# Block-sparse attention with a SoLU feed-forward: moving transposes from TensorE to the DMA crossbar, and the feed-forward to tokens on partitions

## The chip, the cores and the metric

The kernel runs on one core of one Trainium2 chip. The metric is the device time of one execution in microseconds (us), lower is better; the profile's span, from the first to the last instruction, is about 1.7 us shorter. Engines are named as in the profile: PE is TensorE (PEld its weight load), DVE is VectorE, ACT is ScalarE, POOL is GpSimd, SP is SyncE, here the issuer of most DMAs. A run counts as slow when it is more than 1.5 % above the fastest of its kernel. Ratios are those formed from fast runs of the same rounds.

## The reference

```python
# q, k, v: (4 batches, 8 heads, 768 tokens, 64), block = 32
scores = scale * q @ k^T                        # 768 x 768 for each head
scores = where(mask, scores, -1e9)              # window of 1 block, first and last block, 3 random blocks a row
attn   = softmax(scores) @ v
x      = attn, heads side by side               # (3072 tokens, 512)
h      = x @ w_in                               # (3072, 1024)
solu   = h * softmax(h)                         # over the 1024
ln     = (solu - mean) / sqrt(var + 1e-6) * g_ln
out    = ln @ w_out                             # (3072, 512)
```

## The kernel before

Heads go through in pairs ("pr"), queries in tiles of 256 ("t"), so there are 48 attention units, each of three groups of four score matmuls. The mask is added by the score matmul itself: 24 more contraction rows hold block indicators in kT and mask values in qT. One feed-forward ("feed") follows every four units. A small planner inside the kernel simulates the engines with rough costs, decides the order of all operations, and emits them in that order. On the chip each engine then runs its own list in order. `take` draws a buffer from a pool, `last_of` gives it back, `due` is a priority.

The k and q path before: GpSimd casts, TensorE transposes, VectorE copies out of PSUM.

```python
ca = op(e, us, cast, [ld], due=due, take=mp, last_of=[ld])           # e is POOL but for the first pair
def tp(o, cb=cb, ca=ca):
    for c in range(NCH):                                             # 6 transposes by PE
        nc.tensor.matmul(t[:, c * P : (c + 1) * P], cb[ca.slot][:, c], ident, is_transpose=True, ...)
t = op("PE", NCH * 0.056, tp, [ca, mids], due=due, take="m", last_of=[ca])
...
got.append(op(e2, ..., cp, [t, prev], due=due + 0.1, ...))           # PSUM -> kT or qT, one copy a head
```

The feed-forward before: the 1024 features of h lie on partitions, so solu needs no transpose for the output matmul, but the sums over features become 48 narrow matmuls a feed.

```python
xp = op("PE", 2 * KD * 0.056, xpose, x_done[(b, t)], ...)            # x transposed by PE
for f2 in range(KF // 2):                                            # four times
    h  = op("PE",  8 * 0.1088, hmm, [xc, w_in_load], take="m", ...)  # w_in stationary, tokens moving
    e  = op("ACT", act_us(512), ... func=ACT.Exp ...)
    so = op("DVE", dve_us(512), ... tensor_mul ...)                  # solu
    sqs.append(op("DVE", dve_us(512, 2), ... tensor_mul ...))        # squares
st = op("PE", 48 * 0.0256, stats, es + sos + sqs, ...)               # sums of e, solu, solu^2 by matmuls with ones
om = op("PE", KF * 0.2156, outp, sos + wo, ...)                      # twice
```

w_out is prepared on the chip. Eight VectorE operations `wg` scale it by g, TensorE sums its columns (`cs`), and eight more VectorE operations `wo` subtract the mean `wbar`. Every output matmul waits for `wo`.

The softmax here doesn't subtract the row's maximum and nothing guards it: scores larger than these inputs give would overflow.

Of the kernel before, what the change touches and what calls it, by code (L numbers as in the profile page):

```python
# [7 lines left out]
FP32 = mybir.dt.float32  # L8
# [24 lines left out]
class Op:  # L33
    def __init__(self, eng, us, emit, deps, due, take=None, last_of=(), load=None, after=()):
        self.eng, self.us, self.emit, self.due = eng, us, emit, due
        self.deps = [d for d in deps if d is not None]
        self.after = list(after)
        self.take = take
        self.last_of = list(last_of)
        self.load = load  # L40
        self.slot = None
        self.start = None
        self.seen = None


class Plan:


    def __init__(self):
        self.ops = []  # L50
        self.pools = {}
        self.free = {e: 0.8 for e in SEEN}
        self.dma_free = 0.0

    def pool(self, name, n):
        self.pools[name] = [0.0] * n

    def op(self, eng, us, emit, deps=(), due=0.0, take=None, last_of=(), load=None, after=()):
        o = Op(eng, us, emit, deps, due, take, last_of, load, after)
        self.ops.append(o)  # L60
        return o

    def place(self, o, wait=0.03):

        t = 0.0
        for d in o.deps:
            if d.seen is None:
                return INF, None
            t = max(t, d.seen)
        for d in o.after:  # L70
            if d.start is None:
                return INF, None
            t = max(t, d.start)
        slot = None
        if o.take is not None:
            slots = self.pools[o.take]
            slot = min(range(len(slots)), key=lambda k: (slots[k], k))
            t = max(t, slots[slot])
        return t, slot

    def run(self):
        todo = {e: [] for e in SEEN}
        for o in self.ops:
            todo[o.eng].append(o)
        order = []
        while any(todo.values()):
            best = None
            for e, ops in todo.items():
                if not ops:
                    continue  # L90
                now = self.free[e]
                pick = None
                for o in ops:
                    t, slot = self.place(o)
                    if t == INF:
                        continue
                    key = (max(t, now), o.due) if t > now + 0.02 else (now, o.due)
                    if pick is None or key < pick[0]:
                        pick = (key, o, slot, max(t, now))
                if pick is not None and (best is None or pick[3] < best[3]):  # L100
                    best = pick
            assert best is not None, "nothing can be placed"
            _, o, slot, t = best
            todo[o.eng].remove(o)
# [3 lines left out]
            if o.load is not None:  # L108
                self.dma_free = max(self.dma_free, t + 1.0) + o.load
                o.seen = self.dma_free + 1.3  # L110
            if o.take is not None:
                o.slot = slot
                self.pools[o.take][slot] = INF
            for a in o.last_of:
                self.pools[a.take][a.slot] = o.seen
            order.append((t, len(order), o))
        order.sort(key=lambda r: r[:2])
# [4 lines left out]
def kernel(  # L122
# [19 lines left out]
    NT = 3  # L142
# [8 lines left out]
    eps_ln = 1e-6  # L151

# [3 lines left out]
    NST, NKB, NEX, NX, NE, NSO, NSQ, NXT, NOT = 3, 3, 9, 6, 2, 3, 2, 2, 3  # L156

    def bufs(name, shape, dt, n):
        return [const.tile(shape, dt, name=f"{name}{i}") for i in range(n)]

    kT = bufs("kT", [P, 2, NPR, S], BF16, 2)
    qT = bufs("qT", [P, 2, NPR, S], BF16, 2)
# [4 lines left out]
    kb = bufs("kb", [P, NCH, 2, D], BF16, NKB)  # L167
    qb = bufs("qb", [P, NCH, 2, D], BF16, NKB)
    exb = bufs("ex", [P, 4, TW], BF16, NEX)
    xb = bufs("x", [P, 2, d_model], BF16, NX)  # L170
    xTb = bufs("xT", [P, KD, 2, P], BF16, NXT)

    eso = const.tile([P, NE + NSO, KF, TW], BF16, name="eso")
    eb = [eso[:, i] for i in range(NE)]
    sob = [eso[:, NE + i] for i in range(NSO)]
    sqall = const.tile([P, NSQ, KF, TW], BF16, name="sqall")
    sqb = [sqall[:, i] for i in range(NSQ)]
    w_out_f = (eso.rearrange("p a b c -> p (a b c)")[:, 0 : 2 * KF * d_model]
               .bitcast(FP32).rearrange("p (c d) -> p c d", c=KF))
    w_out_g = sqall.rearrange("p a b c -> p (a b c)").rearrange("p (c d) -> p c d", c=KF)  # L180
    otb = bufs("ot", [P, d_model], FP32, NOT)
    rb = bufs("r", [P, 2, 2, 1], FP32, 2)
    s3b = bufs("s3", [P, 2, 3], FP32, 2)
    s2b = bufs("s2", [P, 2, 2], FP32, 2)
    v2b = bufs("v2", [P, 2], FP32, 2)
    rsb = bufs("rs", [P, 2], FP32, 2)
# [5 lines left out]
    st_sel = const.tile([P, 1, 3], FP32, name="st_sel")  # L192
    neg_half = const.tile([P, 2], FP32, name="neg_half")
# [3 lines left out]
    sbank = [psum.tile([P, 4, TW], FP32, name=f"sbank{i}") for i in range(2)]  # L197
    mbank = [psum.tile([P, 2, TW], FP32, name=f"mbank{i}") for i in range(4)]

    plan = Plan()  # L200
    plan.pool("s", 2)
    plan.pool("m", 4)
    for nm, n in (("kst", NST), ("qst", NST), ("vst", NST), ("kb", NKB), ("qb", NKB), ("ex", NEX),
                  ("x", NX), ("xT", NXT), ("e", NE), ("so", NSO), ("sq", NSQ), ("ot", NOT),
                  ("r", 2), ("s3", 2), ("s2", 2), ("v2", 2), ("rs", 2)):
        plan.pool(nm, n)
    op = plan.op
    LOAD = 2 * P * NCH * D * 4 / 330e3

    def bank(o, shape=None, dt=FP32):  # L210
        t = mbank[o.slot].rearrange("p a b -> p (a b)")
        return t if dt == FP32 else t.bitcast(dt)


    samp_i = const.tile([1, NB * NR, 2], I32, name="samp_i")
    _t = sampled_blocks.tensor
    _t32 = bass.DRamTensorHandle(_t.name, (2 * NB * NR,), I32)
    maskT = const.tile([NB, NB], FP32, name="maskT")
    ones1 = const.tile([1, NB], BF16, name="ones1")
    samp_lo = const.tile([1, NB * NR], BF16, name="samp_lo")  # L220
    kb_iota_i = const.tile([NB, 1], I32, name="kb_iota_i")
    kb_iota = const.tile([NB, 1], FP32, name="kb_iota")
    eq = const.tile([NB, NB, NR], FP32, name="eq")
    anyeq = const.tile([NB, NB], FP32, name="anyeq")
    sel = const.tile([NB, NB, BLK], BF16, name="sel")
    mskb = const.tile([NB, NB, BLK], BF16, name="mskb")
    selp = const.tile([NB, 1, S], BF16, name="selp")
    mskp = const.tile([NB, 1, S], BF16, name="mskp")

    samp_dma = op("ACT", 0.06, lambda o: nc.scalar.dma_start(  # L230
        out=samp_i.rearrange("a b c -> a (b c)"),
        in_=bass.AP(tensor=_t32, offset=0, ap=[[0, 1], [1, 2 * NB * NR]])), due=-100, load=0.01)

    warm = const.tile([1, 1], FP32, name="warm")
    w0 = op("DVE", 0.1, lambda o: nc.vector.memset(warm, 0.0), due=-99)
    op("ACT", 1.4, lambda o: nc.scalar.activation(out=warm, in_=warm, func=ACT.Exp), [w0], due=-99)
    stage = {}

    loads = []

    def load(b, pr, which):
        src, dst, nm = {"k": (k, kst, "kst"), "q": (q, qst, "qst"), "v": (v, vst, "vst")}[which]
        stage[(which, b, pr)] = op("SP", 0.08, lambda o: nc.sync.dma_start(
            out=dst[o.slot].rearrange("p h c d -> p h (c d)"),
            in_=src[b, 2 * pr : 2 * pr + 2].rearrange("h (p c) d -> p h (c d)", p=P)),
            due=-50 + len(loads), take=nm, load=LOAD, after=loads[-1:])
        loads.append(stage[(which, b, pr)])

    for b in range(B):
# [4 lines left out]
    m0 = op("DVE", 0.38, lambda o: nc.vector.memset(kT[0][0:D, 1, 0, :], 0.0), due=-90)  # L254
    m1 = op("DVE", 0.38, lambda o: nc.vector.memset(qT[0][0:D, 1, 0, :], 0.0), due=-89)
    mid = op("POOL", 0.15, lambda o: nc.gpsimd.memset(ident, 0.0), due=-95)
    mids = op("POOL", 0.35, lambda o: nc.gpsimd.affine_select(
        out=ident, in_=ident, compare_op=ALU.not_equal, fill=1.0, base=0, channel_multiplier=1,
        pattern=[[-1, P]]), [mid], due=-94)
    last = op("POOL", 0.1, lambda o: nc.gpsimd.memset(maskT, 0.0), due=-93)  # L260
    for base, cm, pat, fill in ((1, -1, [[1, NB]], NEG), (1, 1, [[-1, NB]], NEG),
                                (-1, 1, [[0, NB]], 0.0), (NB - 2, -1, [[0, NB]], 0.0),
                                (-1, 0, [[1, NB]], 0.0), (NB - 2, 0, [[-1, NB]], 0.0)):
        last = op("POOL", 0.25, lambda o, base=base, cm=cm, pat=pat, fill=fill:
                  nc.gpsimd.affine_select(out=maskT, in_=maskT, compare_op=ALU.is_ge, fill=fill,
                                          base=base, channel_multiplier=cm, pattern=pat),
                  [last], due=-92)
    static_mask = last
    ms = op("DVE", 0.38, lambda o: nc.vector.memset(sel, 0.0), due=-96)
    sels = op("POOL", 1.0, lambda o: nc.gpsimd.affine_select(  # L270
        out=sel, in_=sel, compare_op=ALU.not_equal, fill=1.0, base=0, channel_multiplier=1,
        pattern=[[-1, NB], [0, BLK]]), [ms], due=-91)
    io = op("POOL", 0.15, lambda o: nc.gpsimd.iota(kb_iota_i, pattern=[[0, 1]], base=0,
                                                  channel_multiplier=1), due=-92.5)
    io2 = op("DVE", 0.1, lambda o: nc.vector.tensor_copy(out=kb_iota, in_=kb_iota_i), [io], due=-85)
    on1 = op("DVE", 0.1, lambda o: nc.vector.memset(ones1, 1.0), due=-88)
# [337 lines left out]
```

## Time and profile before

| | before |
|---|---|
| time, median of 4 runs | 258.74 us (257.24 to 260.01) |
| span and mean granted clock of the profiled run (fast) | 255.2 us, 0.99 |
| PE, DVE, ACT busy | 223.4, 159.3, 175.7 us |
| first score matmul | 16.95 us |

These are the first table and three rows of slices from the page of the kernel before. Each digit is the busy share of one fortieth of the span in tenths. PEclk is the granted TensorE clock.

```profile
PE 223.4 (88%) x3155; PEld 182.7 (72%) x3177; DVE 159.3 (62%) x329; ACT 175.7 (69%) x210; POOL 66.8 (26%) x120
...
PE   0539778984999999999999999999999999999692
...
ACT  3218899696548958588686884877959688686331
...
PEclk9999999998899999999999999999999999999998
```

The next lines are the table of stretches of the same run: stretch, its length, then for each engine busy us and instruction count, then the clock, the DMA share and GB/s.

```profile
50.00:60.00 10.00, 7.41 (x122) 6.43 (x119) 9.78 (x15) 7.76 (x8) 5.79 (x6) 1.00 1.07 372
60.00:70.00 10.00, 8.20 (x102) 7.30 (x100) 7.33 (x18) 5.42 (x7) 2.05 (x2) 0.83 0.47 147
70.00:130.00 60.00, 59.63 (x875) 49.31 (x880) 38.51 (x83) 44.08 (x55) 16.29 (x29) 1.00 0.22 73
130.00:190.00 60.00, 59.63 (x879) 49.73 (x884) 36.30 (x84) 45.01 (x56) 6.90 (x18) 1.00 0.08 31
```

From 70 us on PE is full (59.63 of 60) and everything else has room, the DMA engines most. Before 70 us PE has gaps. These groups of the page show the work that the change touches (line, engine, operation, output<-input, count | busy us, mean ns | idle before it, and what ended most of that), and the queue that SP feeds:

```profile
q1 hardware_dynamic: 19024, 27.86, 33.2%
...
L431 ACT ACTIVATE ex<-sbank 128x1024 bf16<-128x1024 f32 x144 | 141.9, 1026 | 45.7 <-PE sbank L425 44.9
...
L502 ACT ACTIVATE eso<-mbank 128x512 bf16<-128x512 f32 x48 | 28.8, 602 | 9.3 <-PE mbank L494 9.3
...
L510 DVE TENSOR_TENSOR sqall<-eso 128x512 bf16<-128x512 bf16 x48 | 21.1, 446 | 0.9
...
L399 DVE COPY qT<-mbank 64x768 bf16<-64x768 bf16 x31 | 17.1, 553 | 2.2 <-PE mbank L383 1.7
L399 DVE COPY kT<-mbank 64x768 bf16<-64x768 bf16 x32 | 17.6, 550 | 1.0 <-PE mbank L383 0.5
```

### The profile page before, as it was taken

What the parts mean: (1) busy time and instruction counts of PE and PEld (TensorE: products, weight loads), DVE (VectorE), ACT (ScalarE), POOL (GpSimd) and SP (SyncE); (2) the same over time, 40 slices, a digit from 0 to 9 for tenths busy, and PEclk for the clock granted to TensorE, in tenths of its full rate; (3) what the DMA queues carried; (4) which work ended last, traced back from release to release, by engine and by line L of the source; (5) the groups of instructions that cost most, each with busy time, mean ns of one, the idle gap of its engine ahead of it and who ended that gap; (6) DMA issues with size and microseconds to landing.
All of it is one profiled execution on the core that took longest, in us unless ns stands there. A gap on an engine that the chain in (4) does not pass through costs nothing.

```text
span 255.2 us, 7442 instructions
## 1 busy us (share of the span) xinstructions
PE 223.4 (88%) x3155; PEld 182.7 (72%) x3177; DVE 159.3 (62%) x329; ACT 175.7 (69%) x210; POOL 66.8 (26%) x120
## 2 busy tenths in 40 slices
PE   0539778984999999999999999999999999999692
PEld 0317666673887879889788796987969778787461
DVE  7999634999584759568438395862735428263361
ACT  3218899696548958588686884877959688686331
POOL 8883325773051222142303101001010100101001
PEclk9999999998899999999999999999999999999998
DMA  6999999999234041022110200202002020100202
GB/s 193 378 303 251 361 289 295 372 373 312 66 109 161 5 154 52 3 83 66 42 45 3 82 3 9 78 0 85 3 3 83 3 85 0 74 15 3 82 0 85
DMA packets 19587, 29.39 MB, mean 115 GB/s; under 512 B 2273, under 2 KB 14946, under 8 KB 19554
## 3 DMA queue, kind: packets, MB, share of 16 engines
q1 hardware_dynamic: 19024, 27.86, 33.2%
q0 software_dynamic: 528, 1.05, 2.2%
q8 instruction: 25, 0.41, 0.7%
q14 instruction: 8, 0.07, 0.1%
q10 hardware_dynamic: 2, 0.00, 0.0%
HBM read 23.07 MB, written 6.29 MB: 115 GB/s over the span
## 4 chain that ended last, share of the span: by engine, by line
PE 73%; DVE 16%; ACT 6%; issue 2%; POOL 1%; POOLq 0%; ACTq 0%
PE sbank L425 21%; PE mbank L494 15%; PE mbank L547 14%; PE mbank L442 12%; PE mbank L520 6%; ACT ex L431 5%; PE mbank L383 3%; DVE w_out_sb L354 3%; DVE sqall L343 2%; PE mbank L476 2%; DVE kT L399 2%; DVE qT L399 1%; DVE mskp L298 1%; DVE kT L320 1%; DVE eso L506 1%
## 5 line engine op out<-in xcount | busy, mean ns | idle before, releaser
L431 ACT ACTIVATE ex<-sbank 128x1024 bf16<-128x1024 f32 x144 | 141.9, 1026 | 45.7 <-PE sbank L425 44.9
L425 PE MATMUL sbank<-qT,kT 128*128 128x256 bf16 (+1 forms) x576 | 84.3, 277 | 11.3 <-ACT ex L431 5.6
L425 PEld LDWEIGHTS <-kT 128*128 128x128 bf16 (+1 forms) x576 | 53.7, 99 | 23.6 <-issue 14.6
L494 PE MATMUL mbank<-xT,w_in_sb 128*128 128x256 bf16 x384 | 48.1, 273 | 0.8 <-DVE xT L480 0.8
L442 PE MATMUL mbank<-va,ex 128*128 128x65 bf16 x1152 | 44.4, 195 | 2.9 <-DVE qT L399 1.8
L442 PEld LDWEIGHTS <-ex 128*128 128x128 bf16 x1152 | 42.7, 98 | 4.9 <-issue 2.4
L506 DVE TENSOR_TENSOR eso<-mbank,eso 128x512 bf16<-128x512 f32 x48 | 32.7, 687 | 20.0 <-ACT eso L502 19.6
L547 PE MATMUL mbank<-w_out_sb,eso 128*128 128x512 bf16 x170 | 43.4, 379 | 1.7 <-DVE eso L506 0.5
L494 PEld LDWEIGHTS <-w_in_sb 128*128 128x128 bf16 x384 | 36.7, 97 | 5.1 <-issue 0.9
L502 ACT ACTIVATE eso<-mbank 128x512 bf16<-128x512 f32 x48 | 28.8, 602 | 9.3 <-PE mbank L494 9.3
L452 DVE RECIPROCAL r<-mbank 128x4 f32<-128x4 f32 x48 | 8.5, 178 | 38.1 <-PE mbank L442 37.9
L532 POOL TENSOR_TENSOR s<-s 128x4 f32<-128x4 f32 x12 | 2.5, 212 | 109.5 <-DVE s L528 109.5
L547 PEld LDWEIGHTS <-eso 128*128 128x128 bf16 x192 | 18.0, 97 | 18.1 <-DVE eso L506 1.2
L374 POOL CAST kb<-kst 128x768 bf16<-128x768 f32 x15 | 13.5, 898 | 51.3 <-PE mbank L383 30.7
L510 DVE TENSOR_TENSOR sqall<-eso 128x512 bf16<-128x512 bf16 x48 | 21.1, 446 | 0.9
L455 DVE TENSOR_TENSOR x<-mbank,r 128x256 bf16<-128x256 f32 x48 | 20.1, 421 | 1.2
L405 POOL CAST va<-vst 128x768 bf16<-128x768 f32 x16 | 15.1, 941 | 14.2 <-PE mbank L442 9.3
L399 DVE COPY qT<-mbank 64x768 bf16<-64x768 bf16 x31 | 17.1, 553 | 2.2 <-PE mbank L383 1.7
L399 DVE COPY kT<-mbank 64x768 bf16<-64x768 bf16 x32 | 17.6, 550 | 1.0 <-PE mbank L383 0.5
L559 ACT ACTIVATE ot<-mbank,rs 128x512 f32<-128x512 f32 x12 | 8.2, 687 | 11.3 <-POOL rs L541 5.3
L374 POOL CAST qb<-qst 128x768 bf16<-128x768 f32 x15 | 13.1, 876 | 5.6 <-PE mbank L383 3.1
L556 DVE TENSOR_SCALAR ot<-mbank,rs 128x512 f32<-128x512 f32 x12 | 9.0, 750 | 8.8 <-POOL rs L541 7.2
(63 smaller groups left out, 153.5 us busy)
## 6 DMA issues: line engine op xcount, KB each, us to landing
kst<-in_k_dram SPq DMA_DIRECT2D x16, 384.0 KB, 7.2
qst<-in_q_dram SPq DMA_DIRECT2D x16, 384.0 KB, 7.8
vst<-in_v_dram SPq DMA_DIRECT2D x16, 384.0 KB, 8.5
out_dram<-ot SPq DMA_DIRECT2D x24, 256.0 KB, 2.0
eso<-in_moe_w_out_dram SPq DMA_DIRECT2D x1, 2048.0 KB
w_in_sb<-in_moe_w_in_dram POOLq DMA_DIRECT2D x1, 1024.0 KB, 12.4
kT<-selp SPq DMA_DIRECT2D x2, 144.0 KB
qT<-mskp SPq DMA_DIRECT2D x2, 144.0 KB
```

The source lines that it names most:

```text
L374: (nc.vector if o.eng == "DVE" else nc.gpsimd).tensor_copy(out=cb[o.slot], in_=src)
L399: nc.vector.tensor_copy(out=d_, in_=s_)
L425: nc.tensor.matmul(s[:, m, :], kT[i][rows[hh], hh, pr, jc * P : (jc + 1) * P], qT[i][rows[hh], hh, pr, t * TW : (t + 1) * TW], start=(m % ...
L431: exs.append(op("ACT", act_us(1024), lambda o, so=so: nc.scalar.activation(out=exb[o.slot], in_=sbank[so.slot], func=ACT.Exp, scale=scale) ...
L442: nc.tensor.matmul(acc[:, qt, hh, :], exb[exs[n].slot][:, m, qt * P : (qt + 1) * P], va[i][:, 2 * pr + hh, jc, :], start=first, stop=(n == ...
L455: nrm = op("DVE", dve_us(TW), lambda o: nc.vector.tensor_tensor(out=xb[x_of[(b, t)].slot][:, :, 2 * pr * D : (2 * pr + 2) * D].rearrange(" ...
L494: nc.tensor.matmul(h[:, ff, :], w_in_sb[:, c, f * P : (f + 1) * P], xTb[xc.slot][:, c].rearrange("p a q -> p (a q)"), start=(ff == 0 and c ...
L502: e = op("ACT", act_us(512), lambda o, h=h, sl=sl: nc.scalar.activation(out=eb[(es[0] if es else o).slot][:, sl, :], in_=mbank[h.slot], fu ...
L506: so = op("DVE", dve_us(512), lambda o, h=h, sl=sl: nc.vector.tensor_mul(out=sob[(sos[0]).slot][:, sl, :], in0=mbank[h.slot], in1=eb[es[0] ...
L510: sqs.append(op("DVE", dve_us(512, 2), lambda o, sl=sl: nc.vector.tensor_mul(out=sqb[sqs[0].slot][:, sl, :], in0=sob[sos[0].slot][:, sl, : ...
L520: nc.tensor.matmul(s3p[:, qt, g : g + 1], t_[:, f, qt * P : (qt + 1) * P], onesf[:, 0:1], start=first, stop=(qt == 1 and g == 2 and f == K ...
L547: nc.tensor.matmul(bank(o), sob[sos[0].slot][:, f, qt * P : (qt + 1) * P], w_out_sb[:, f, :], start=(f == 0), stop=(f == KF - 1))
```

## The change

The intent is to take transposes and sums off the full TensorE and give them to engines with room. For batches 1 to 3 the crossbar of the DMA engines transposes q and k; for all feeds but the last it transposes x and solu. Batch 0 stays with TensorE, because its data is needed at once. h is computed with tokens on partitions. Then exp gives its row sum as it runs (`accum_out`), `bn_stats` gives the variance, and the statistics matmuls and squares go; but solu now needs a transpose. h gets a PSUM pair of its own. The mask is built token-major beside k and q, so that one transpose brings both for batch 0. The core of the diff, cut:

```diff
-    plan.pool("s", 2)
-    plan.pool("m", 4)
+    plan.pool("s", 2, "sh")
+    plan.pool("h", 1, "sh", 2)                  # "m" has 2 banks now
 ...
-            t = op("PE", NCH * 0.056, tp, [ca, mids], due=due, take="m", last_of=[ca])
+            if b:
+                ca = op("POOL", pool_us(S), cast, [ld], due=due, take=nm + "b", last_of=[ld])
+                x = op("SP", xbar_us(48), lambda o, cb=cb, ca=ca: nc.sync.dma_start_transpose(
+                    out=half(cb[ca.slot], 1).rearrange("p (c q) -> p c q", c=NCH), in_=half(cb[ca.slot], 0)),
+                    [ca], due=due - 200, load=48 * TILE)
+                for hh in range(2):
+                    got[hh].append(op("DVE", dve_us(S, 4), ... nc.vector.tensor_copy(
+                        out=dst[i][0:D, pr, hh, :], in_=half(cb[ca.slot], 1)[hh * D : hh * D + D, :]),
+                        [x, prev] + (wo if b == 1 and pr > 1 else []), due=due, last_of=[ca]))
 ...
-        xp = op("PE", 2 * KD * 0.056, xpose, x_done[(b, t)], ...)
+            xp = op("SP", xbar_us(64), lambda o: nc.sync.dma_start_transpose(
+                out=xTb[o.slot]..., in_=xb[x0.slot]...), x_done[(b, t)], due=F[0] - 200, take="xT", ...)
+        for a in range(2):                      # 128 tokens each
+            h = op("PE", 2 * 0.2156, hmm, [xp, w_in_load], take=None if n else ("sh" if late else "h"), ...)
+            se = op("ACT", act_us(d_ff) + 0.23, ... func=ACT.Exp, accum_out=seb[...])
+            so = op("DVE", dve_us(d_ff), ... tensor_mul ...)
+            bn = op("DVE", 2 * dve_us(512), ... bn_stats ...)
-        st = op("PE", 48 * 0.0256, stats, es + sos + sqs, ...)
+                st = op("SP", xbar_us(64), lambda o, so=so: nc.sync.dma_start_transpose(
+                    out=sotb[o.slot], in_=sob[so.slot]), [so] + wo, ..., take="soT", load=64 * TILE, last_of=[so])
 ...
-    w_out_load = op("SP", 0.08, ... nc.sync.dma_start(out=w_out_f, ...)
+    w_out_load = [op("POOL", 0.82, lambda o, i=i: nc.gpsimd.dma_start(out=hold[i], ...), [loads[10]], ...) for i in range(3)]
```

## The prediction

> **What bounds it now.** TensorE. In the table of 10-us stretches PE is 98-100% busy from 70 to 230 us at clock 1.00; the chain of waits is 73% PE. Back-to-back rates from the timeline: a score group of 4 matmuls 0.44 us, PV of one unit (24) 0.75, 8 matmuls of h 0.87, 8 output matmuls 1.73 (216 ns each; the Trainium skill, "TensorE: Matmul & The Clock Gate", back-to-back issue gap, gives N/2.4+2.5 ns, the same), statistics 1.18, six transposes 0.34. Summed: scores 63.4, PV 36, h 42, output 41.5, statistics 14, q/k transposes 10.8, x transposes 5.4, weights 1.7: 215 of the 255 us span. The other 40: the first scores start at 16.95 (mask copies on DVE: 1.7, 2.8, 1.3 us, wait "qT L308" 5.2 us), 20-70 us waits on ACT exps and on 13.6 us of w_out preparation on DVE, and a tail after 236.
>
> **What changes.**
> 1. PE: statistics gone (-14.2); q, k transposes of batches 1-3 gone, batch 0 now 96 of them (-5.4); x transposes only in the last feed, which adds 16 for solu (-4.1). h keeps its stream (192 x 216 ns = 41.5). New sum, an estimate: about 191 us, minus 24.
> 2. ACT: 144 exps at 0.985 us stay (142); 24 exps of 128x1024 with row sum replace 48 of 0.60, about 1.25 each by estimate (30 for 28.8); output scaling leaves (-8.2). About 175: now nearly as loaded as PE.
> 3. DVE: squares (21), x copies (8.2) and 24-row mask copies go; bn_stats (about 29), 12 more output scalings (9) come; 96 copies of q, k become 48 from SBUF, about 0.27 us each by estimate, plus batch 0. Total near 155.
> 4. DMA: 24 transposes of 192 KB and 33 of 256 KB. The skill, "DMA: Bandwidth & Descriptors", latency table, states 261 GB/s effective: 0.75 and 1.0 us of movement by estimate, plus landing; no trace here shows it. Output stores took 2.0 us to land, so I estimate 3-4 us per transpose. With three soT buffers and about 7.5 us per half feed this hides in steady state.
> 5. PSUM: one pair for h. It is held for h (1.73, stretched by interleaving to about 3), exp (up to 1 wait + 1.25) and the product on DVE (wait + 1.2): about 7 us by estimate, against a period of 7.6 us per half. Tight.
> 6. Start: no long 24-row copies between mask and scores; I expect the first score near 10-11 us instead of 17.
>
> **Path.** Nearly all of the PE removal is on the path from 70 to 230: a period (four units, one feed) falls from 17.7 to 15.2 us of PE work. ACT needs 14.2 of it, so some comes back as waits between two nearly full engines: I allow 5%. Start 11, PE 191/0.95 = 201, idle in the exp-bound batch 0 about 3, tail about 6: span about 220, runs a little over.
>
> **Time: 222 us, 80% range 210 to 236.** Faster by over 2% 0.95, within 0.03, slower 0.02.
>
> **What would show it.** PE groups for statistics gone, busy near 195; first score before 12 us; PE share still above 90% from 60 to 195, with new idle ended by ACT (ex) or by the h product; DMA transposes landing in under 4 us; q, k copies near 0.27 us.
>
> **What would make it wrong.** Transposes slow or blocking the in-order SP queue (loads behind a waiting transpose); the single h pair over 7.6 us; then PE gaps appear before h and out. Below 210 if ACT and PE interleave perfectly.

## The result, and the profile after

The first four runs gave a median of 236.88 us (233.38 to 237.89); six more in the last experiment gave 236.16 us (233.37 to 237.63). Two of the four and two of the six were slow. The six fast runs of both sets lie between 233.37 and 236.19 us, with a median of 235.6; this is the time that later comparisons use. The ratios are not quite those of the quoted medians. The first ratio to before is 0.907 (95 % interval 0.893 to 0.921), the second 0.919 (0.914 to 0.923). "Faster" was right. The median of the first four lies 0.9 us above the stated range, that of the fast runs just inside it; against the point of 222 us the kernel is 14 us too slow.

The profiled one of the first four runs was slow (span 236.2 us, clock 0.963). The lines below come from the fast profile of the last experiment, which ran the same kernel (span 231.7 us, clock 0.985). Both show the same stall. The page of the changed kernel, the same parts as before:

```profile
PE 204.6 (88%) x2277; PEld 144.1 (62%) x2308; DVE 149.2 (64%) x320; ACT 166.7 (72%) x199; POOL 65.5 (28%) x142
...
PE   6989880997897999999988999999999899999973
...
ACT  3196893499688788888985978889887889763200
...
PEclk9999996799999999999999999999999999999999
...
q1 hardware_dynamic: 71840, 39.14, 72.8%
...
L485 ACT ACTIVATE ex<-sbank 128x1024 bf16<-128x1024 f32 x144 | 139.1, 1035 | 35.7 <-PE sbank L478 35.2
...
L562 DVE TENSOR_TENSOR eso<-sbank,eso 128x1024 bf16<-128x1024 f32 x24 | 29.2, 1217 | 11.4 <-ACT eso L559 11.2
L559 ACT ACTIVATE eso<-sbank 128x1024 bf16<-128x1024 f32 x24 | 24.9, 1038 | 9.7 <-issue 3.2
L565 DVE BATCH_NORM_STATS2 bn<-eso 128x6 f32<-128x512 bf16 x48 | 30.7, 681 | 0.3
...
L412 DVE COPY kT<-kb 64x768 bf16<-64x768 bf16 x24 | 9.9, 411 | 14.2 <-DMA kb<-kb 13.8
```

The first score now starts at 11.56 us. In the steady part PE is nearly as full as before, with less to do:

```profile
35.00:50.00 15.00, 9.43 (x110) 6.98 (x111) 8.04 (x24) 8.06 (x10) 1.66 (x2) 0.77 0.69 135
50.00:60.00 10.00, 7.54 (x97) 5.44 (x97) 9.89 (x18) 8.69 (x11) 2.34 (x3) 1.00 0.83 227
60.00:70.00 10.00, 9.90 (x119) 7.14 (x118) 7.09 (x19) 8.25 (x10) 3.75 (x7) 1.00 1.10 223
70.00:130.00 60.00, 55.39 (x637) 38.71 (x646) 39.23 (x87) 49.16 (x59) 22.29 (x41) 1.00 1.11 239
130.00:190.00 60.00, 57.55 (x633) 39.97 (x642) 38.31 (x81) 49.77 (x61) 12.16 (x28) 1.00 0.61 128
```

But from 35 to 50 us PE is busy 9.43 of 15 us, at 0.77 of its clock. The timeline of VectorE and then of PE in that stretch (start us, length, instruction, and in brackets the idle time before it and what ended it):

```profile
27.53 0.42 DVE L509 TENSOR_TENSOR x<-mbank,r 128x256 bf16<-128x256 f32 x1
37.21 0.72 DVE L412 COPY kT<-kb 64x768 bf16<-64x768 bf16 x2 [9.26 <-DMA kb<-kb]
...
39.72 1.27 DVE L370 TENSOR_SCALAR w_out_sb<-kT,g_sb 128x512 bf16<-128x512 f32 x3
```

```profile
34.18 0.60 PE L478 MATMUL sbank<-qT,kT 88*128 88x256 bf16 x4 [0.32 <-ACT ex L485]
40.24 0.58 PE L376 MATMUL mbank<-w_out_sb,onesf 128*128 128x512 bf16 x1 [5.46 <-DVE w_out_sb L370]
40.62 1.52 PE L495 MATMUL mbank<-va,ex 128*128 128x65 bf16 x24
```

VectorE stood 9.26 us in front of the first kT copy of batch 1. Behind that copy in its list stood two normalizations of finished PV results (PV is the product of exps and v) and the scaling of w_out. TensorE's next matmul in its list, the column sum `cs`, needs a scaled piece of w_out, and by the trace this scaling ended its wait of 5.46 us. The data to be scaled were there before: the three loads of w_out landed at 31.9, 35.0 and 36.6 us, and the scaling began at 39.72. ScalarE's next exp in the trace waited 6.21 us. Then TensorE came back at half clock. The Trainium skill, "TensorE: Matmul & The Clock Gate", "What's actually happening", says that a monitor halves the clock after an idle window of about 3.4 us and restores it after a busy one. The trace agrees in part. Its clock was half from 37.1 to 43.9 us, until 3.7 us after TensorE came back; this is the 6 and 7 of the PEclk row. But the half clock began only 2.3 us after the end of the last matmul, and in experiment 5 an idle time of 2.85 us was followed by half clock too (53.2 to 56.6 us). So less than 3.4 us of idle time was enough here.

To see where the time lies I count TensorE's work in each stretch, from the weight loads in the trace times the back-to-back intervals of the timeline (score 0.11 us, PV 0.031, h and output 0.216, transposes 0.056; matmuls that only warm up TensorE at the start are left out), and call the rest of the stretch lost. This sum is mine, not a line of the profile.

| us | before | predicted | after, fast profile | after, first profile (slow) |
|---|---|---|---|---|
| work | 214.7 | 191 | 191.1 | 191.1 |
| lost, 0 to 20 | 17.1 | 11 | 11.7 | 12.0 |
| lost, 20 to 70 | 14.3 | 3 + 2.5 | 13.3 | 19.3 |
| lost, 70 to 210 | 0.4 | 7 | 8.9 | 7.2 |
| lost, 210 to the end | 8.6 | 6 | 6.7 | 6.5 |

(The 5 % that the prediction allowed on 191 us is 10 us; it is spread here over 20 to 210 us by length, 2.5 and 7.) The work, the start, the steady part and the tail came out within 2 us of what was predicted in the fast profile. The stretch from 20 to 70 us lost 13.3 in place of 5.5. Theory P: it is one head-of-line block on VectorE, and the DMA behind it landed late. Rivals: contention of the weights' traffic or their queue (Q), the tail (T), the h pair, or a shortage that any repair would only move.

### The profile page after: what moved, and what is told of

Its sections match the earlier page's. It is cut to its first block, busy times and chain, and to the rows that moved or that the text cites. A ratio compares the mean times of both kernels' runs of the same rounds, so it can differ in the third digit from the quotient of the medians.

```text
span 236.2 us, 5785 instructions
## 1 busy us (share of the span) xinstructions
PE 207.8 (88%) x2277; PEld 146.1 (62%) x2308; DVE 149.2 (63%) x320; ACT 166.5 (70%) x199; POOL 65.8 (28%) x142
## 5 line engine op out<-in xcount | busy, mean ns | idle before, releaser
L478 PE MATMUL sbank<-qT,kT 88*128 88x256 bf16 x576 | 84.1, 276 | 5.8 <-ACT ex L485 5.0
L478 PEld LDWEIGHTS <-kT 88*128 88x128 bf16 x576 | 52.9, 98 | 26.6 <-issue 10.5
L550 PE MATMUL sbank<-w_in_sb,xT 128*128 128x512 bf16 x172 | 49.5, 388 | 2.7 <-DVE eso L562 1.6
L562 DVE TENSOR_TENSOR eso<-sbank,eso 128x1024 bf16<-128x1024 f32 x24 | 29.2, 1216 | 11.5 <-ACT eso L559 11.3
L559 ACT ACTIVATE eso<-sbank 128x1024 bf16<-128x1024 f32 x24 | 24.8, 1035 | 9.7 <-issue 3.2
L565 DVE BATCH_NORM_STATS2 bn<-eso 128x6 f32<-128x512 bf16 x48 | 30.7, 681 | 0.3
L550 PEld LDWEIGHTS <-xT 128*128 128x128 bf16 x192 | 19.1, 100 | 13.9 <-issue 3.5
L600 DVE TENSOR_SCALAR ot<-mbank,rs 128x512 f32<-128x512 f32 x24 | 17.8, 741 | 9.6 <-PE mbank L590 7.2
L412 DVE COPY kT<-kb 64x768 bf16<-64x768 bf16 x24 | 9.3, 387 | 15.8 <-DMA kb<-kb 15.6
L461 POOL CAST va<-vst 128x768 bf16<-128x768 f32 x16 | 13.6, 848 | 14.7 <-DMA vst<-in_v_dram 14.7
L575 POOL TENSOR_TENSOR rs<-mv,neg_half 128x1 f32<-128x1 f32 x24 | 13.7, 572 | 1.8
L402 POOL CAST kb<-kst 128x768 bf16<-128x768 f32 x12 | 10.0, 835 | 13.4 <-DMA kst<-in_k_dram 13.4
## 6 DMA issues: line engine op xcount, KB each, us to landing
kT<-in_moe_w_out_dram POOLq DMA_DIRECT2D x1, 768.0 KB, 18.6
```

Source lines behind the costliest of these rows:

```text
L402: nc.gpsimd.tensor_copy(out=half(cb[o.slot], 0).rearrange("p (c h d) -> p c h d", c=NCH, h=2), in_=st[ld.slot].rearrange("p h c d -> p c h ...
L478: nc.tensor.matmul(s[:, m, :], kT[i][0:DM, pr, hh, jc * P : (jc + 1) * P], qT[i][0:DM, pr, hh, t * TW : (t + 1) * TW], start=(m % 2 == 0), ...
L550: nc.tensor.matmul(h[:, f * 512 : (f + 1) * 512], xTb[xp.slot][:, a, c, :], w_in_sb[:, c, f * 512 : (f + 1) * 512], start=(c == 0), stop=( ...
L559: se = op("ACT", act_us(d_ff) + 0.23, lambda o, h0=h0: nc.scalar.activation(out=eb[o.slots["e"]], in_=pair(h0), func=ACT.Exp, accum_out=se ...
L562: so = op("DVE", dve_us(d_ff), lambda o, h0=h0, se=se: nc.vector.tensor_mul(out=sob[o.slot], in0=pair(h0), in1=eb[se.slots["e"]]), [se], d ...
L565: bn = op("DVE", 2 * dve_us(512), lambda o, so=so: [nc.vector.bn_stats(out=bnb[o.slot][:, f], in_=sob[so.slot][:, f * 512 : (f + 1) * 512] ...
```

## The experiments

Twelve runs, each checked against the reference. All gave correct results but the first, which is wrong. "Replanned" marks edits after which the kernel's planner chose another order for all engines: such a run compares two whole schedules. "Frozen" means that all engines but the one named keep their order exactly.

### 1. The weights made without DMA (replanned, wrong)

```diff
-    w_in_load  = op("POOL", 0.82, ... nc.gpsimd.dma_start(out=w_in_sb, ...), load=6.0)
+    w_in_load  = op("POOL", 2.2, ... nc.gpsimd.memset(w_in_sb..., 0x3C003C00), ...)
-    w_out_load = [op("POOL", 0.82, ... nc.gpsimd.dma_start(out=hold[i], ...), load=2.0) ...]
+    w_out_load = [op("POOL", 1.6, ... nc.gpsimd.memset(hold[i], 0.01), ...) ...]
```

> w_in and w_out are filled by memsets on GpSimd instead of 4 MB of DMA (wrong result on purpose); everything else, the order rules included, stays. Theory W (the weights' transfers, issued by GpSimd at 15 to 19 us, hold up the DMA engines, so that the first two crossbar transposes take 5.3 and 9.4 us to issue and land at 39 us): both then issue in under 2 us and land in under 7 us, the 10.8 us DVE wait before L412 and the half-clock stretch at 38-48 us go, and the time falls by 9 to 12 us to about 224-228. Rival O (transposes are slow to issue beside any queued load of q, k, v, and the weights do not matter): the two still take over 4 us each to issue and the time stays within 3 us of the changed kernel's 233-238.

Measured: 228.94 us (228.54 to 229.57), ratio to before 0.884. The longest wait for a k transpose is 2.7 us, the transposes issue in 1.2 to 2.3 us each, and the slowest of the first ones lands after 8.1 us. The time lies 0.9 us above what theory W expected, but the wait it named is gone. So without the 3 MB of weights in their way the transposes land in time. It doesn't say whether the shared queue or the mere volume holds them up, and the memsets cost time of their own at 12 to 20 us (5.2 us lost there, 1.9 in the fast profile of the changed kernel).

### 2. The planner told that the first transpose lands 9 us later (replanned)

```diff
-                    [ca], due=due - 200, load=48 * TILE)
+                    [ca], due=due - 200, load=48 * TILE + (9.0 if b == 1 and pr == 0 and nm == "k" else 0.0))
```

> Same instructions and same transfers; the planner is only told that the first transpose of batch 1 lands 9 us later, so VectorE gets the copies out of it behind the PSUM evictions of batch 0 and the first scalings of w_out. Theory P (the late landing costs time only because the in-order VectorE stands before these copies with evictions behind them): the 10.8 us VectorE wait shrinks to what the w_out scalings wait for their own data (landing at 36-39 us), and the time falls by 4 to 8 us to 228-232. Rival W alone (nothing after 36 us can go on before the DMA backlog is gone, whatever the order): within 2 us of 233-238.

Measured: 239.51 us (238.97 to 240.53), no gain. The stall is gone: 9.3 us lost from 20 to 70 us. But the new plan loses 17.8 us from 70 to 190, where the kernel as changed loses 6.3 and 8.4 in its two profiles. The costliest wait there is the same fault in batch 2:

```profile
96.12 0.74 DVE L412 COPY kT<-kb 64x768 bf16<-64x768 bf16 x2 [6.22 <-DMA kb<-kb]
```

This run is a miss for me, and a caution: an edit to a planned kernel changes everything after it. The next tests of theory P had to freeze the order.

### 3. Batch 1 also by TensorE (replanned)

```diff
-            if b:
+            if b > 1:                     # batch 1 takes the TensorE path of batch 0, casts on POOL
```

> q and k of batch 1 also go through TensorE (96 more 128-column transposes of 0.056 us, so +5.4 us of PE work; masks come with them), the crossbar starts with x and batch 2. If the stall at 35-50 us is owed to the first crossbar transposes (W or P), it goes (about -10 us) and PE work gives about 5 back: 228-233. If the stall is owed to w_out preparation or loads alone: the stall stays and the time rises to 238-242.

Measured: 241.11 us (239.81 to 241.68). The time is the one expected for "the stall stays", and yet the stall is gone: 35 to 50 us loses 3.1 us, where the fast profile of the changed kernel loses 7.3. TensorE's work rises by 5.4 us to 196.5, and a new wait for kT copies of 5.5 us appears at 48.5 to 54.0 us, with half clock at its end. In it VectorE is busy with the w_out subtractions, which stand in front of these copies in its list; no DMA is involved. So the time decides between neither expectation, and giving up the crossbar for batch 1 is no cure.

### 4. The last output scalings on ScalarE (replanned)

```diff
-            fo = op("DVE", dve_us(512), fin, [om, rs], ...)
+            fo = op("ACT" if late else "DVE", act_us(512) if late else dve_us(512), fin, [om, rs], ...)
```

> The six output scalings of the last three feeds go from VectorE to ScalarE. Theory T (after the last attention unit VectorE is the limit: 99.7% busy from 220 to 230 us, with ScalarE at 22%): six times 0.74 us leave VectorE, time falls by 2 to 4 us to 231-234. Rival: the tail is bound by the chain of the last half feed and TensorE (99% busy from 210 to 220): under 1 us.

Measured: 236.69 us (235.93 to 237.16). The tail lost 6.2 us against 6.5 and 6.7. Taking six scalings from VectorE in the last feeds gains at most half a microsecond; rival T falls.

### 5. Eight copies moved on VectorE, all else frozen

```diff
+                    if b == 1 and pr < 2:
+                        early.append(got[hh][-1])            # the 8 kT and qT copies of pairs 0 and 1
 ...
     order = plan.run()
+    order = [o for o in order if o not in early]
+    at = min(order.index(s) for s in first_b1)               # before the first score of batch 1
+    order[at:at] = sorted(early, key=lambda o: o.start)
```

> The order of every engine is that of the changed kernel, checked instruction by instruction; only the eight copies of the first two pairs of batch 1 stand later on VectorE, just before the first use by a score. Theory P (the in-order VectorE before late transposes is what stalls the kernel at 35-43 us): PSUM evictions go on, what is left is the wait for w_out itself (landing 36-39 us), so TensorE resumes near 37 instead of 42.2 us; the time falls by 4 to 7 us to 229-232, and since the rest of the order is unchanged nothing is given back. Rival G (ground gained here is given back later, as in e2, by the DMA supply of later batches): under 2 us, 234-237.

Measured: 226.97 us (226.31 to 227.18), all four runs fast, ratio to before 0.880 (0.874 to 0.887). The first transposes issue in 4.6 and 7.9 us and land at about 38 us, late as ever; nothing about the DMA was mended. Only what stands behind the copies changed. The stretches of this run, then the scaling of w_out and the first kT copy on VectorE, then on TensorE the first column sum and the one long wait that is left there:

```profile
35.00:50.00 15.00, 13.22 (x184) 9.90 (x181) 11.31 (x24) 14.15 (x17) 3.69 (x5) 1.00 1.19 228
50.00:60.00 10.00, 7.89 (x80) 5.87 (x83) 7.38 (x20) 6.20 (x8) 3.01 (x5) 0.83 1.14 218
...
70.00:130.00 60.00, 56.96 (x659) 40.05 (x668) 40.94 (x92) 49.96 (x60) 22.83 (x41) 1.00 1.10 238
```

```profile
33.30 1.37 DVE L370 TENSOR_SCALAR w_out_sb<-kT,g_sb 128x512 bf16<-128x512 f32 x3
...
50.88 0.73 DVE L412 COPY kT<-kb 64x768 bf16<-64x768 bf16 x2
```

```profile
34.54 0.38 PE L376 MATMUL mbank<-w_out_sb,onesf 128*128 128x512 bf16 x1
...
52.05 0.61 PE L480 MATMUL sbank<-qT,kT 88*128 88x256 bf16 x4 [2.85 <-DVE qT L412]
```

PE is busy 13.22 of 15 us at full clock where it had 9.43 at 0.77, and ScalarE 14.15 where it had 8.06. The 20 to 70 us stretch loses 8.9 us. The scaling begins at 33.30 us in place of 39.72, and the column sum at 34.54 in place of 40.24. This settles theory P: the place of the copies in VectorE's in-order list was worth about 9 us (235.6, the median of the six fast runs, less 226.97; 4 % by the ratios, 0.880 over 0.919). I had expected 4 to 7, because I took w_out to land too late for more. The Trainium skill, "TensorE: Matmul & The Clock Gate", paragraph "Engine queue depths", calls the queues of VectorE and ScalarE strict FIFO; both traces agree, 9.26 us of waiting with ready work behind it in the one and no wait before the same copies in the other.

### 6. w_out on the SP queue, ahead of the transposes (frozen)

```diff
+    def g_and_w_out(o):                   # SP issues w_out right after g; POOL issues nothing for it
+        g_only(o)
+        for i in range(3):
+            nc.sync.dma_start(out=hold[i], in_=moe_w_out...)
```

> Same bytes, same order of all engines; the 2 MB of w_out are issued by SyncE right after g, on the queue that also carries the loads and the transposes, instead of by GpSimd on its own queue. Theory Q (two queues share the DMA engines[...]): the first two transposes issue in under 3 us each and land by 28-32 us, the wait of L412 falls from 10.8 to under 4 us, time 226-231. Rival V (volume: all of it has to pass before 36 us in any order): the transposes still land at 35-39 us, time 233-238.

Measured: 236.54 us (234.78 to 238.05), all fast. The transposes now issue in at most 2.3 us each and land within 6.6 us. But they start later, k at 28.1 us and q at 33.5. SP first has the weights to issue (11.7 to 17.1 us) and then, by the trace, waits 2.9 us for a load of w_out to land; the q transpose waits for its q load, which landed at 32.5. The first copy waits no less than before, 11.5 us (in the line: us in total, times, longest):

```profile
DVE kT L419 <- DMA kb<-kb: 18.1, 7, 11.5
```

So moving the bulk of the weights to the same queue (w_in, 1 MB, stayed on its own) doesn't get the first transpose there sooner. Half of rival Q's expectation held, the short issues; the earlier landing and the gain did not. The sharing between two queues falls as the main cause. With experiment 1 this leaves the volume that stands ahead of the transposes at 20 to 37 us, on whichever queue. Two views of the changed kernel show it. First the transpose of k in that stretch (its issue in ns, 5.4 us, its start, and its landing after 16.3 us), then the DMA table cut to 24 to 36 us:

```profile
L407 SPq DMA_TRANSPOSE kb<-kb x1: 5393/5393/5393, 20.9 to 20.9; - x1
...
DMA to landing us min/median/max: 16.3/16.3/16.3
```

```profile
DMA packets 1934, 3.55 MB, mean 296 GB/s; under 512 B 695, under 2 KB 1199, under 8 KB 1932
...
q0 software_dynamic: 753, 2.46, 72.4%
q1 hardware_dynamic: 1179, 1.05, 34.1%
```

In those 12 us the weights' queue moved 2.46 MB in 753 packets. Of the transposes' packets (256 bytes each, by the trace) at most 695 went through, under 0.2 MB: less than one transpose of 192 KB. The packets of the trace show where they stood: not one of 256 bytes started before 30 us. SP's queue was still moving the k and q loads issued ahead of the transposes, at 18.7 and 19.4 us, and these landed at 30.2 and 33.7 us beside the weights. So the transposes stood behind late loads in their own queue as well. The Trainium skill, "DMA: Bandwidth & Descriptors", § Queues, rings and completion order, says that each DMA engine turns between its queues packet by packet. By that the small packets of the transposes would lose to packets of 3 KB, if the trace's packets are the page's. The counts fit it, but no run here varied the packet size, so this part is argued, not shown.

### 7. The planner counts transposes behind queued loads (replanned)

```diff
-                self.xbar_free = max(self.xbar_free, t + 1.0) + o.load * (1.4 if self.dma_free > t + 1 else 1.0)
-                self.dma_free = max(self.dma_free, t) + o.load
-                o.seen = self.xbar_free + 1.3
+                self.xbar_free = self.dma_free = max(self.dma_free, t + 1.0) + o.load
+                o.seen = self.dma_free + 1.3
```

> The planner counts a crossbar transpose as queued behind the loads already issued, as the trace shows it; nothing else changes, but the whole order is planned anew. If late landings against an optimistic plan are the cause: the VectorE waits for transposed kb, qb fall from 16.4 us in total to under 5, no half-clock stretch between 30 and 200 us, time 227-232. If any new plan just moves the waits (as e2): 235-240.

Measured: 231.99 us (230.34 to 233.28), ratio 0.900. A plan that knows of the queue avoids the long wait by itself: the waits for k transposes are no longer among VectorE's largest. One stretch of half clock is left (35.0 to 38.4 us), where I had expected none. It gives part back in waits of scores for exps, 10.7 us in all, where experiment 5 has 3.7.

### 8. x and solu by TensorE in every feed (replanned)

```diff
-        feed(b, t, [...], j == B * NT - 1, j >= B * NT - 3)
+        feed(b, t, [...], True, j >= B * NT - 3)
```

> Undoes one part: x and solu of all feeds by TensorE and VectorE copies instead of the crossbar (q, k of batches 1-3 stay on it). TensorE work +14.9 us (33 more groups of 0.45), VectorE +22 us, crossbar load falls from 57 to 24 transposes. If the crossbar pays for x and solu as predicted: 244-250. If the transposes' DMA time (73% of the 16 engines) is what holds the steady part back: 232-240. Planned anew, so an effect of plan as in e2 (3 us) can lie on top.

Measured: 259.36 us (257.34 to 260.37), ratio to before 1.006. Tokens on partitions with the transposes of x and solu left on TensorE gain nothing over the kernel before. The crossbar for these two is worth about 24 us (259.4 less 235.6): 14.8 us of TensorE work (205.9 against 191.1), and a tail that loses 13.4 us in place of 6.5 and 6.7. I had expected 244 to 250, and had not counted the tail.

### 9. The copies moved again, four of them earlier (frozen)

```diff
+    at = min(order.index(s) for s in first_b1)
+    order[at:at] = late4                                       # pair 1: before the first score of batch 1
+    at = sorted(order.index(w) for w in wo)[4]
+    order[at:at] = [o for o in early if o not in late4]        # pair 0: before the fifth w_out subtraction
```

> Same instructions and the same order on TensorE, ScalarE, GpSimd and SyncE as the changed kernel; of the eight k/q copies of batch 1, the four of pair 0 now stand among the eight w_out subtractions (before the fifth), the four of pair 1 just before the first score of batch 1. In the run that put all eight there, TensorE waited 2.85 us at 52 us for a q copy and the time was 227.0. Theory P (only the place of the copies in the VectorE stream costs): the 2.85 us wait before the first score of batch 1 falls below 1 us and the time is 224 to 226, ratio to before 0.868 to 0.878. Rival (the wait was hiding another one: exps or free score pairs, or the other four copies): another wait of 1 to 3 us opens within 10 us of it and the time stays 226 to 228.

Measured: 228.13 us (225.76 to 231.76, two of six slow; 227.2 is the median of the fast ones), ratio to before 0.880, the same as in experiment 5. The rival's expectation held. The 2.85 us wait went, and two others came within 2 us of it:

```profile
50.41 0.60 PE L482 MATMUL sbank<-qT,kT 88*128 88x256 bf16 x4 [1.32 <-DVE w_out_sb L383]
52.14 1.86 PE L556 MATMUL sbank<-w_in_sb,xT 128*128 128x512 bf16 x4 [1.13 <-DVE eso L568]
```

At 42 to 56 us VectorE has the w_out subtractions, the copies, the first solu product and the first `bn_stats` to do almost without a break. Which of them goes first hardly matters there.

### 10. h without its own pair, copies moved (replanned)

```diff
-        feed(b, t, [...], j == B * NT - 1, j >= B * NT - 3)
+        feed(b, t, [...], j == B * NT - 1, True)               # h, scores and batch 0 transposes all take "sh"
```

> The own PSUM pair taken away: h draws from the same three pairs as the scores everywhere (the pool that the changed kernel uses only in the first and last feeds), with the eight copies of batch 1 moved as in the run of 227.0 us, against which it is compared. Theory S (the own pair is what lets h and scores interleave): h takes the pair that the next score needs, or waits behind scores; 3 to 8 us more lost between 70 and 210 us, 230 to 235 us. Rival (three shared pairs serve as well, since a pair is a pair and the order is planned anyway): 225 to 229 us.

Measured: 235.28 us (231.93 to 238.79, two of four slow), ratio 0.904 against 0.880 of experiment 5: 2.7 % slower, as theory S expected (the two fast runs took 231.93 and 234.94 us). The profile is of a slow run, though one with a clock of 0.984, so its sums are less sure: 15.3 us are lost from 70 to 210 where experiment 5 loses 7.1. VectorE's products wait 25.1 us in all for the exps of h, against 11.2 us in experiment 5:

```profile
DVE eso L566 <- ACT eso L563: 25.1, 13, 3.7
```

The own pair pays, though the run compares two plans. That one pair was "tight", as the prediction had it, cost little: TensorE waits for the product in all 1.4 us (three times) in the changed kernel.

### 11. x and solu by TensorE, with the copies moved (replanned)

This is experiment 8 with the edit of experiment 5.

> x and solu by TensorE in all feeds (259.4 us with the copies left in place) and the eight copies of batch 1 moved. Theory A (the stall of batch 1 and the work of the feed's transposes are separate costs that add): the 7.4 us wait of TensorE for the w_out scaling goes and the time falls by 8 to 11 us, to 248 to 252. Rival (with the fuller TensorE the stall was partly covered, or the tail takes it back): 253 to 258.

Measured: 254.16 us (252.82 to 254.79), ratio 0.985. Moving the copies gains 5 us here, not the 8 to 11 that I expected: the rival was nearer. The wait of 7.4 us for the w_out scaling did go, but 50 to 60 us now loses 4.1 us (2.1 in experiment 8). Against experiment 5 the crossbar for x and solu is worth 27 us.

### 12. The changed kernel again, unedited

> The changed kernel itself, unedited, six more runs: two of its first four were of the slow state, and so was the profiled one. If the stall of VectorE belongs to the kernel and not to the slow state, a fast profile shows it too: VectorE waits 10 to 12 us for the first kT copy of batch 1, TensorE 6 to 8 us for the w_out scaling, and the median of the fast runs is 234 to 238, within 1 % of the 236.5 of the run with w_out on the other queue. If it belongs to the slow state, the fast runs are at 226 to 230 and the wait is under 3 us.

Measured: 236.16 us (233.37 to 237.63, four of six fast), ratio 0.919. The fast profile has the stall, 9.3 us on VectorE and 5.5 us on TensorE (a little under what I wrote). It does not belong to the slow state. The two profiles of the kernel, at 231.7 and 236.2 us, differ most from 20 to 70 us: in the slower one the stall is longer (10.8 us on VectorE, 7.0 on TensorE) and a second stretch of half clock follows at 61.5 to 68.3 us.

## Why the prediction was right or wrong

- **TensorE's work, right.** Predicted 191 us, counted 191.1. The per-operation rates of the kernel before carried over: h took 384 matmuls of 109 ns and now takes 192 of 216 ns, about 41.5 us both times, which is the N/2.4+2.5 ns of the skill's page that the prediction cited. The profile's busy time, which models the ends of matmuls and includes half clock, is 204.6 us where "near 195" was written.
- **The start, right, a little late.** Predicted "near 10-11", measured 11.56 and 11.79 us; the 5.2 us wait for long mask copies is gone.
- **ScalarE and the exps, right in kind.** The row sum costs 1038 + 215 ns a piece, as estimated (1.25 us). The sum of 175 was too high: 166.7 us busy.
- **Steady part and tail, right in size, the steady part partly by luck.** 8.9 us lost from 70 to 210 where 5 % allowed 7; 6.7 in the tail where 6 was written. But the prediction had put the steady loss down to exps and the h product. In the fast profile these ended 1.6 and 0.7 us of TensorE's waits from 70 to 210; the longest item was the landing of solu transposes, 2.4 us in two waits, which the prediction had held to be hidden.
- **The copies of q and k, wrong but small.** Predicted 0.27 us each, measured 0.41 and 0.39 us: 48 copies cost 19.2 us in place of 13. VectorE still came out at 149 us, under the 155 written.
- **Transposes, right in steady state, wrong at the start.** Median landings of 3.9 (solu), 4.0 (q) and 4.3 us (x) about meet "3-4 us"; of the 12 k transposes the trace gives two landings, 3.1 us and the first, 16.3 (18.6 in the first profile). The time on the DMA engines was mis-sized by the cited figure: from 261 GB/s the prediction had 0.75 and 1.0 us each, 51 us for all 57. The share of SP's queue rose from 33.2 % to 72.8 %, and the transposes' own packets (13.37 MB, 256 bytes each) took 84.1 us of all 16 engines in the fast profile and 87.9 in the first. With 57 transposes in 230 us this still fitted.
- **The step that failed** is the sum's "idle in the exp-bound batch 0 about 3". It is the term that was mis-sized: the stretch from 20 to 70 us lost 13.3 us in the fast profile and 19.3 in the slow one, with 5.5 allowed for it (3, and 2.5 of the general 5 %). The exp-bound part itself, 20 to 35 us, lost only 2.8. The rest is the transition to batch 1: first crossbar data, w_out preparation, first feed. The prediction had named "waits on ACT exps and on 13.6 us of w_out preparation on DVE" as a cost of this stretch in the kernel before, which lost 14.3 us there. The sixteen VectorE operations for w_out are all still there (13.6 us before, 10.3 in the fast profile after), and yet they were left out of the new sum. The change then put eight VectorE copies that wait for a DMA in front of it and between it, four of them before the first scaling.
- **"Transposes slow or blocking the in-order SP queue" was the right worry about the wrong queue.** SP's first two issues were slow (5.4 and 6.3 us where 1.2 is usual), but what cost the time was VectorE's list behind the data. Experiment 5 took that away alone and gained about 9 us with the DMA as late as before; at 226.97 us it stands 5 us from the point prediction, and still loses 8.9 us from 20 to 70 us.
- What stays open is why the planner's small moves in the steady part cost what they cost (experiments 2 and 7 changed everything at once), and whether packet size or bytes alone slow the first transposes.

The best version found is that of experiment 5: 226.97 us, 4 % under the changed kernel and 12 % under the one before.

## What to carry to other kernels

When work moves from a full engine to the DMA, its arrival becomes a wait at the head of some other engine's in-order list: ask what stands behind it there, above all at the start, when the weights are still on their way. Put the consumer of a late transfer just before its first use, not where a planner's guess says the data lands. And when a prediction names a cost in the old kernel, it stays in the new sum unless a line of the change removes it.

## What the Trainium skill lacked or had wrong

- "DMA: Bandwidth & Descriptors", latency table: 261 GB/s for a DMA transpose with a non-contiguous middle dimension. One rate does not fit here. A 256 KB transpose of solu with nothing beside it (fast profile, at 210 us) started all its packets within 1.4 us, about 190 GB/s; in the densest microsecond of the same profile, at 109 us and with two transposes in flight, 287 GB/s of transpose packets started.
- The same page has no figure for a transpose beside a large load: the first one landed after 16.3 us (18.6 in the slow profile) where about 4 us is usual, and the first two took 5.4 and 6.3 us to issue on SP (5.3 and 9.4) where 1.2 us is usual, while 3 MB of weights were in flight. With no weights by DMA the slowest of the first ones took 8.1 us.
- No page was found that gives the cost of an exp's row sum: the separate read of the accumulator took 215 ns after each exp of 1038 ns.
